# Layer 1's first nine hidden slices with their clip split between ScalarE and GpSimd, and a third score slot kept for one unit more

## The chip, the cores and the metric

The kernel runs on one core of a Trainium2 chip. The metric is device microseconds of one execution. The kernel before was timed three times: 1115.95 us is the median, 1115.87 and 1116.27 are the ends.

## The reference, cut to what matters

```python
# attention, 4 batches x 8 heads, 576 positions, head size 64
scores = scale * q @ k.T
scores = where(scores >= rowmax - tau, scores, -1e9)
attn   = softmax(scores)                  # then attn @ v, heads side by side: x is 2304 x 512
# layer 1, 512 -> 2048 -> 512
h = x @ w_in
g = where(h >= 1, h, where(h <= -1, 0, (h + 1) ** 2 / 4))
x = g @ w_out
# layer 2, 512 -> 2048 -> 512
r = maximum(x @ w_in2, 0);  g = s * r * r + b;  out = g @ w_out2
```

All is float32. Large matrix products are made of three passes over a high and a low part of each operand.

## The kernel before, in words

**Attention** is walked in 32 units: a unit is one half of the query rows of one pair of heads in one batch, so a batch has eight units, the four of the first half and then the four of the second. A unit of the first half has four score tiles (128 queries x 576 keys), one of the second half has five, so a batch has 36 tiles. For each tile TensorE makes the scores (line 515 in batches 0 and 1, where four matmuls run on quarters or halves of the array at once, called tiled below; line 524 in batches 2 and 3). VectorE takes the row minimum of the negated scores (570), ScalarE the exponential (573), VectorE masks and sums (578). The row sums go through some short instructions (591 to 597, on GpSimd or VectorE), one of GpSimd, VectorE and ScalarE normalises the tile (608, 613), TensorE transposes it (634, 650), ScalarE or VectorE copies it out (626, 627), and at the end of a row block the values are multiplied in (672, 673).

**Layer 1 beside attention.** The weights of ten of layer 1's sixteen slices of 128 hidden rows are brought in and split during the first 200 us: a chunk takes an Abs on ScalarE (816), a clamp on GpSimd (819), three bit operations on VectorE (822, 824, 826), a cast on ScalarE (828) and a subtraction on GpSimd (493). As soon as a group of 256 or 320 tokens has its attention output, some of its slices are computed between the score tiles: 3 for the first group, 7 for the second, then 10 for each of four more. A slice is twelve matmuls into a PSUM bank (898), the activation, a cast to the high part (918, ScalarE) and the low part (919, GpSimd); four output sums (941) use the slices of a group. The activation of a slice h is `c = clip(h, -1, 1)` on VectorE (906), `c = ((c + 1) / 2) ** 2` on ScalarE (908), `hs = max(c, h)` on VectorE (910).

**PSUM.** There are eight banks. Score tiles take two, as (0,1), (2,3) and, for the units below `ALONE`, (6,7) as well; these last two are `ps3_117` in the lists. Transposes and values use 4 and 5. From unit `ALONE` on, 6 and 7 are two banks of their own (`ps4_0`, `ps4_1`) for values, hidden slices and output sums. The first group's slices use them before that.

**Order.** Every operation is a task with a priority. A list scheduler in the kernel walks the tasks with its own costs and hop times, picks the engine where a task has alternatives, and writes the five engines' programs out in that order; on the chip each engine works through its list and waits where it has to. `OFF` shifts the priorities of the steps, `BURST` lets TensorE take several tasks of one kind in a row from the planned time `BURST_FROM` on. While TensorE has nothing to do in the plan, before 200 us, and one of the banks 4 to 7 is free, the scheduler puts in a fill: a matmul of the identity with itself (1092), whose result nobody reads.

**Afterwards** all that is left of layer 1 and then layer 2 runs with TensorE as the busy engine (898, 984, 1018).

Of the kernel before, what the change touches and what calls it, by code (L numbers as in the profile page):

```python
# [10 lines left out]
AF = mybir.ActivationFunctionType  # L11
ALU = mybir.AluOpType
# [17 lines left out]

WT0, WT = 0.0, 310.0

OFF = {"load": 0.0, "prep": 0, "qk": -8, "min": -3.0, "exp": -3, "mask": 0, "norm": 0, "trans": 3.58, "hi": 6, "av": 3, "xo": 0, "second": -12}
NSX, NSL, NV = 4, 5, 2

AHEAD = 1
# [12 lines left out]
QKW = 640 + S  # L49
NRH, NHH = 4, 3  # L50

ALONE = 6

BURST, BURST_FROM, BURSTS = 2, 200000.0, ("t", "r")
DMA_ISSUE, DMA_RATE, DMA_LAG = 475, 350.0, 2500.0

DMA_ALONE = 6000.0
# [41 lines left out]
class Sched:  # L99
# [14 lines left out]
    def add(self, alts, prio, r=(), w=(), group=None, lag=0, after=0.0):  # L114

        alts = [a + (True,) if a[0] == "pool" else a for a in alts]
        t = Task()
        t.alts, t.prio, t.idx, t.group, t.lag, t.after = alts, prio, len(self.tasks), group, lag, after
        t.succ, t.npred, t.ready, t.start, t.fn, t.preds = [], 0, 0.0, None, None, []
        preds = {}  # L120
        for k in r:
            p = self.lastw.get(k)
            if p is not None:
                preds[p.idx] = p
        for k in w:
            p = self.lastw.get(k)
            if p is not None:
                preds[p.idx] = p
            for p in self.readers.get(k, ()):
                preds[p.idx] = p  # L130
        for k in r:
            self.readers.setdefault(k, []).append(t)
        for k in w:
            self.lastw[k] = t
            self.readers[k] = []
        for p in preds.values():
            p.succ.append(t)
            t.npred += 1
        if group is not None:
            group.left += 1  # L140
        self.tasks.append(t)
        return t
# [154 lines left out]
def act_ns(n, bias=False):  # L297
    return 93 + n / 1.2 + (94 if bias else 0)
# [7 lines left out]
def dve_ns(n):  # L306
    return 68 + 1.0417 * n


def fast_ns(n):  # L310
    return 68 + 0.521 * n
# [6 lines left out]
def pfast_ns(n):  # L318
    return 60 + 1.07 * n
# [20 lines left out]
def attention_then_ffn(tc, qk, v, tau, w1, w2, s2, b2, out):  # L340
    nc = tc.nc
    sch = Sched()
    add = sch.add
# [538 lines left out]
    def hidden(f, T, xs, layer, cands, gs):  # L882
        pr = prio_f()
        g = Group(cands)
        kg = ("bank", g)
        i = tctr[0]
        tctr[0] += 1
        hs, c = hs_t[i % NH][:, 0:T], c_t[i % NH][:, 0:T]
        khs, kc = ("hs", i % NH), ("c", i % NH)

        def mm():
            o = bank[g.banks[0]][:, 0:T]
            n = 0
            for k in range(4):
                wh, wl = WH[f][:, k * 128:(k + 1) * 128], WL[f][:, k * 128:(k + 1) * 128]
                x_h, x_l = XH[xs][:, k * T:(k + 1) * T], XL[xs][:, k * T:(k + 1) * T]
                for a, x in ((wh, x_h), (wh, x_l), (wl, x_h)):
                    nc.tensor.matmul(o, a, x, start=(n == 0), stop=(n == 11))  # L898
                    n += 1

        add([("pe", 12 * mm_ns(T), mm, "r")], pr, r=["two"] + wkeys(f, 0) + [(t, xs, j) for t in ("XH", "XL") for j in range(4)], w=[kg, "hidden order"] + gs[0] + gs[1], group=g)
        fp = (-1,) + pr
        kgh, kgl, gh, gl = gs
        if layer == 1:

            add([("dve", dve_ns(T), lambda: nc.vector.tensor_scalar(  # L906
                out=c, in0=bank[g.banks[0]][:, 0:T], scalar1=1.0, scalar2=-1.0, op0=ALU.min, op1=ALU.max))], fp, r=[kg], w=[kc], group=g)
            add([("act", act_ns(T, True), lambda: nc.scalar.activation(out=c, in_=c, func=AF.Square, bias=half, scale=0.5))],  # L908
                fp, r=[], w=[kc])
            add([("dve", dve_ns(T), lambda: nc.vector.tensor_tensor(out=hs, in0=c, in1=bank[g.banks[0]][:, 0:T], op=ALU.max))],  # L910
                fp, r=[kc, kg], w=[khs], group=g)
        else:
            add([("act", actp_ns(T), lambda: nc.scalar.activation(out=hs, in_=bank[g.banks[0]][:, 0:T], func=AF.Relu))],  # L913
                fp, r=[kg], w=[khs], group=g)
            add([("act", act_ns(T), lambda: nc.scalar.activation(out=c, in_=hs, func=AF.Square))], fp, r=[khs], w=[kc])  # L915
            add([("dve", fast_ns(T) + 122, lambda: nc.vector.tensor_scalar(out=hs, in0=c, scalar1=s_c, scalar2=b_c, op0=ALU.mult, op1=ALU.add))],  # L916
                fp, r=[kc, "sb"], w=[khs])
        add([("act", act_ns(T), lambda: nc.scalar.copy(out=gh, in_=hs))], fp, r=[khs], w=kgh)  # L918
        add([("pool", pool_ns(T), lambda: nc.gpsimd.tensor_tensor(out=gl, in0=hs, in1=gh.bitcast(F32), op=ALU.subtract)),  # L919
             ("dve", dve_ns(T), lambda: nc.vector.tensor_tensor(out=gl, in0=hs, in1=gh.bitcast(F32), op=ALU.subtract), True)],  # L920
            fp, r=[khs] + kgh, w=kgl)
# [243 lines left out]
```

## Time and profile before

| | |
|---|---|
| median of three runs | 1115.95 us |
| the profiled execution's own time | 1116.18 us |
| its span, first to last instruction | 1114.3 us |
| around the span | 1.9 us |
| busy: PE, PEld, DVE, ACT, POOL | 1099.0, 978.0, 621.0, 723.8, 603.7 us |
| chain that ended last | PE 87%, ACT 5%, DVE 5% |
| granted TensorE clock | 1.00 in all 40 slices |

PE is TensorE's matmuls, PEld its weight loads, DVE is VectorE, ACT is ScalarE, POOL is GpSimd. A row of the trace has a start and a length; an engine can start an instruction a little before the one ahead of it has ended, so on ScalarE and TensorE the distance between two starts, not the length, is what an instruction costs. A float32 matmul that is not split into parts stands as two records, so each fill of the program is two rows of the trace.

### The profile page before, as it was taken

To read this page: it belongs to the slowest core of one execution; us is meant where nothing else is said; L and a number is where in the kernel's file an instruction comes from. 1 tells how busy PE (TensorE), PEld (TensorE's weight loads), DVE (VectorE), ACT (ScalarE), POOL (GpSimd) and SP (SyncE) were. 2 spreads that over 40 slices of the span, in tenths; PEclk is the share of its full clock that TensorE was granted. 3 is DMA by queue.
4 is the path that set the end of the run, shared out by engine and by line. 5 is a ranking of instruction groups with operands and counts; after the bars stand their busy time and mean duration, and the time that the engine had idled before them with its cause. 6 is when DMAs were issued, how large, how long until landed. Compare 5 with 4: busy or idle time off the path is not lost.

```text
span 1114.3 us, 21581 instructions
## 1 busy us (share of the span) xinstructions
PE 1099.0 (99%) x7686; PEld 978.0 (88%) x7686; DVE 621.0 (56%) x1512; ACT 723.8 (65%) x1648; POOL 603.7 (54%) x954
## 2 busy tenths in 40 slices
PE   9899999999999999999999999999999999999998
PEld 6567777889888899899999999999999999999997
DVE  6998998778777665367888786761111111111111
ACT  6999898879877786456666655664544544445443
POOL 4666666778767473166777766772323323323222
PEclk9999999999999999999999999999999999999999
DMA  5645553354334321264456674410101101000000
GB/s 173 184 157 157 161 171 113 110 140 125 112 115 124 101 73 62 76 191 143 148 161 217 199 223 141 140 48 19 39 2 38 34 5 38 2 19 20 1 19 19
DMA packets 75850, 112.01 MB, mean 101 GB/s; under 512 B 7392, under 2 KB 44768, under 8 KB 75744
## 3 DMA queue, kind: packets, MB, share of 16 engines
q1 hardware_dynamic: 75744, 110.65, 32.2%
q8 instruction: 60, 0.98, 0.4%
q14 instruction: 46, 0.38, 0.1%
HBM read 87.03 MB, written 23.59 MB: 99 GB/s over the span
## 4 chain that ended last, share of the span: by engine, by line
PE 87%; ACT 5%; DVE 5%; issue 1%; POOL 1%; DMA 0%; ACTq 0%; POOLq 0%; DVEq 0%
PE ps L898 34%; PE ps L1018 18%; PE ps L984 11%; PE ps L941 7%; PE ps L672 5%; PE ps L634 4%; PE ps L524 3%; PE ps L515 2%; ACT p L613 2%; DVE p L578 1%; PE ps L673 1%; ACT e L573 1%; PE ps L1092 1%; ACT pt L626 1%; DVE stt L570 1%
## 5 line engine op out<-in xcount | busy, mean ns | idle before, releaser
L919 POOL TENSOR_TENSOR g<-hs,g 128x256 fp32r<-128x256 f32 (+1 forms) x272 | 214.1, 787 | 307.7 <-ACT g L918 285.4
L898 PE MATMUL ps<-xh,wh 128*128 128x256 f32 (+1 forms) x1088 | 316.4, 291 | 0.8 <-DVE hs L910 0.4
L898 PE MATMUL ps<-xl,wh 128*128 128x256 f32 (+1 forms) x1088 | 313.7, 288 | 0.0
L898 PE MATMUL ps<-xh,wl 128*128 128x256 f32 (+1 forms) x1088 | 313.7, 288 | 0.0
L916 DVE TENSOR_SCALAR hs<-c,cst 128x256 f32<-128x256 f32 x144 | 65.0, 451 | 313.5 <-ACT c L915 313.5
L898 PEld LDWEIGHTS ps<-xh,wh 128*128 128x128 f32 x1088 | 206.2, 189 | 9.3 <-DVE hs L910 1.6
L898 PEld LDWEIGHTS ps<-xl,wh 128*128 128x128 f32 x1088 | 206.1, 189 | 5.8
L898 PEld LDWEIGHTS ps<-xh,wl 128*128 128x128 f32 x1088 | 206.0, 189 | 0.0
L1018 PE MATMUL ps<-wh,g 128*128 128x512 f32 x576 | 202.9, 393 | 0.0
L918 ACT CAST g<-hs 128x256 fp32r<-128x256 f32 (+1 forms) x272 | 113.7, 418 | 92.1 <-DVE hs L916 62.1
L913 ACT ACTIVATE hs<-ps 128x256 f32<-128x256 f32 x144 | 55.4, 384 | 133.1 <-PE ps L898 131.8
L578 DVE SCALAR_TENSOR_TENSOR p<-ps,stt,e 128x576 f32<-128x576 f32 x144 | 116.0, 813 | 34.3 <-ACT e L573 18.1
L984 PE MATMUL ps<-g,wh 128*128 128x256 f32 (+1 forms) x624 | 127.4, 297 | 0.4 <-DVE ye L994 0.3
L1018 PEld LDWEIGHTS ps<-wh,g 128*128 128x128 f32 x576 | 108.6, 189 | 19.5
L493 POOL TENSOR_TENSOR wl<-wt,wh 128x256 fp32r<-128x256 f32 x128 | 101.2, 795 | 40.0 <-ACT wh L828 39.3
L570 DVE TENSOR_REDUCE stt<-ps 128x1 f32<-128x576 f32 x144 | 105.4, 749 | 22.3 <-PE ps L524 11.4
L1018 PE MATMUL ps<-wl,g 128*128 128x512 f32 x288 | 113.8, 395 | 0.0
L573 ACT ACTIVATE e<-ps,stt 128x576 f32<-128x576 f32 x144 | 105.4, 747 | 9.7 <-DVE stt L570 8.2
L613 ACT ACTIVATE p<-p,stt 128x576 f32<-128x576 f32 (+3 forms) x113 | 92.4, 822 | 22.2 <-DVE stt L597 20.4
L984 PEld LDWEIGHTS ps<-g,wh 128*128 128x128 f32 x624 | 100.0, 189 | 1.7 <-DVE ye L994 1.1
L908 ACT ACTIVATE c<-c,cst 128x320 f32<-128x320 f32 (+1 forms) x128 | 68.6, 537 | 50.4 <-DVE c L906 49.3
L984 PE MATMUL ps<-g,wl 128*128 128x256 f32 (+1 forms) x312 | 92.0, 295 | 0.0
(71 smaller groups left out, 1962.3 us busy)
## 6 DMA issues: line engine op xcount, KB each, us to landing
st<-in_w_dram SPq DMA_DIRECT2D x128, 256.0 KB, 3.7
vr<-in_v_dram SPq DMA_DIRECT2D x32, 320.0 KB, 3.2
r<-in_qk_dram SPq DMA_DIRECT2D x32, 288.0 KB, 2.9
xr<-xT SPq DMA_DIRECT2D x8, 640.0 KB, 6.0
r<-in_qk_dram SPq DMA_DIRECT2D x16, 304.0 KB, 3.9
xr<-y1T SPq DMA_DIRECT2D x9, 512.0 KB, 3.8
out_dram<-yo SPq DMA_DIRECT2D x18, 256.0 KB, 2.0
r<-in_qk_dram SPq DMA_DIRECT2D x16, 272.0 KB, 3.2
```

The source lines that it names most:

```text
L493: return [("pool", pool_ns(n), lambda: nc.gpsimd.tensor_tensor(out=o(), in0=x(), in1=y(), op=op)), ("dve", dve_ns(n), lambda: nc.vector.te ...
L570: add([("dve", 665, lambda: nc.vector.tensor_reduce(out=nm[:, x:x + 1], in_=Sv(), axis=AX.XY, op=ALU.min))], at(pr, "min"), r=[kg], w=[ks[ ...
L573: add([("act", 624, lambda: nc.scalar.activation(out=ev, in_=Sv(), func=AF.Exp, bias=nm[:, x:x + 1], scale=-1.0))], at(pr, "exp"), r=[kg, ...
L578: nc.vector.scalar_tensor_tensor(out=p[:, x * S:x * S + S].rearrange("p (a c) -> p a c", a=2), in0=Sv(), scalar=nthr[:, x:x + 1], in1=ev, ...
L613: nc.scalar.activation(out=p[i:j, o:o + w], in_=p[i:j, a:a + w], func=AF.Identity, scale=rc[i:j, x:x + 1], bias=un[i:j, x:x + 1])
L898: nc.tensor.matmul(o, a, x, start=(n == 0), stop=(n == 11))
L908: add([("act", act_ns(T, True), lambda: nc.scalar.activation(out=c, in_=c, func=AF.Square, bias=half, scale=0.5))], fp, r=[], w=[kc])
L918: add([("act", act_ns(T), lambda: nc.scalar.copy(out=gh, in_=hs))], fp, r=[khs], w=kgh)
L919: add([("pool", pool_ns(T), lambda: nc.gpsimd.tensor_tensor(out=gl, in0=hs, in1=gh.bitcast(F32), op=ALU.subtract)), ("dve", dve_ns(T), lam ...
L941: nc.tensor.matmul(o, a[:, c], x, start=(f == 0 and n == 0), stop=(f == nf - 1 and n == 2))
L984: nc.tensor.matmul(o, a[:, c], x, start=(f == f0 and n == 0), stop=(f == f1 - 1 and n == 2))
L1018: nc.tensor.matmul(o, x[:, c], a[:, 512:1024], start=(f == 0 and n == 0), stop=(f == NF - 1 and n == 2))
```

## The change

Four things change. In the first nine hidden slices (three of the first token group, six of the seven of the second) the activation becomes `c = relu(h / 2 + 1 / 2)` on ScalarE straight from PSUM, `c = min(c, 1)` on GpSimd (or VectorE, which the scheduler takes for none of the nine), `c = c ** 2` on ScalarE, and the same maximum as before on VectorE. `ALONE` goes from 6 to 7, so unit 6 also has the third score slot. The values' priority is shifted by 5.75 places in place of 3. Bursts of the kind "r" (hidden slices, output sums, scores of batches 2 and 3) begin at 100 us of the plan in place of 200.

```diff
-OFF = {..., "trans": 3.58, "hi": 6, "av": 3, "xo": 0, "second": -12}
+OFF = {..., "trans": 3.58, "hi": 6, "av": 5.75, "xo": 0, "second": -12}
-ALONE = 6
+ALONE = 7
+LIGHT = 9
-BURST, BURST_FROM, BURSTS = 2, 200000.0, ("t", "r")
+BURST, BURST_FROM, BURSTS = 2, 100000.0, ("t","r")
...
-            add([("dve", dve_ns(T), lambda: nc.vector.tensor_scalar(
-                out=c, in0=bank[g.banks[0]][:, 0:T], scalar1=1.0, scalar2=-1.0, op0=ALU.min, op1=ALU.max))], fp, r=[kg], w=[kc], group=g)
-            add([("act", act_ns(T, True), lambda: nc.scalar.activation(out=c, in_=c, func=AF.Square, bias=half, scale=0.5))],
-                fp, r=[], w=[kc])
+            if tctr[0] <= LIGHT:
+                add([("act", act_ns(T, True), lambda: nc.scalar.activation(
+                    out=c, in_=bank[g.banks[0]][:, 0:T], func=AF.Relu, bias=half, scale=0.5))], fp, r=[kg], w=[kc], group=g)
+                add([("pool", pfast_ns(T), lambda: nc.gpsimd.tensor_scalar(out=c, in0=c, scalar1=1.0, scalar2=1.0, op0=ALU.min, op1=ALU.mult)),
+                     ("dve", fast_ns(T), lambda: nc.vector.tensor_scalar(out=c, in0=c, scalar1=1.0, scalar2=None, op0=ALU.min), True)],
+                    fp, r=[], w=[kc])
+                add([("act", act_ns(T), lambda: nc.scalar.activation(out=c, in_=c, func=AF.Square))], fp, r=[], w=[kc])
+            else:
+                ...  # the two lines removed above
             add([("dve", dve_ns(T), lambda: nc.vector.tensor_tensor(out=hs, in0=c, in1=bank[g.banks[0]][:, 0:T], op=ALU.max))],
                 fp, r=[kc, kg], w=[khs], group=g)
```

The four together let the scheduler write another order from the fifth unit on. Three places show it. In the lists of the changed kernel line numbers are 2 higher than before up to the activation (517 for 515, 636 for 634) and 11 higher behind it (952 for 941, 1103 for 1092).

TensorE in units 5 and 6 of batch 0, before: `ps_117` (banks 6 and 7) goes from the scores to the first hidden slice, between the scores of unit 5 and those of unit 6.

```order
L650 MATMUL ps_1_113<-ident,p_121 128x128
L1092 MATMUL ps_0_112<-ident 128x128 x2
L898 MATMUL ps_117<-xh_89,wh_69 128x256
...
L672 MATMUL ps_0_112<-pt,vr_135 64x320 x8
L673 MATMUL ps_0_112<-pl,vr_135 128x320
L634 MATMUL ps_1_113<-ident,p_122 128x128 x4
L515 MATMUL ps_0_110<-r_131 128x288 x2
L515 MATMUL ps_1_111<-r_132 128x288 x2
L898 MATMUL ps_117<-xh_89,wh_70 128x256
```

The same place in the changed kernel:

```order
L652 MATMUL ps_1_113<-ident,p_121 128x128
L1103 MATMUL ps_0_112<-ident 128x128 x2
L517 MATMUL ps_117<-r_131 128x288 x2
L674 MATMUL ps_0_112<-pt,vr_135 64x320 x8
L675 MATMUL ps_0_112<-pl,vr_135 128x320
L636 MATMUL ps_1_113<-ident,p_122 128x128 x4
L517 MATMUL ps_0_110<-r_132 128x288 x2
L517 MATMUL ps_1_111<-r_131 128x288 x2
L636 MATMUL ps_0_112<-ident,p_122 128x128 x4
```

The third slot takes a score tile of unit 6, and the three slices of the first token group (36 matmuls of line 898) stand some twenty rows later, among the scores of units 6 and 7; the sums that use them move with them.

TensorE at the first scores of batch 1 (unit 8), before: fills stand between transposes and scores.

```order
L634 MATMUL ps_1_113<-ident,p_122 128x128 x4
L1092 MATMUL ps_1_1056<-ident 128x128 x5
L650 MATMUL ps_0_112<-ident,p_122 128x128
L1092 MATMUL ps_1_1056<-ident 128x128
L634 MATMUL ps_1_113<-ident,p_120 128x128 x4
L1092 MATMUL ps_1_1056<-ident 128x128 x2
L634 MATMUL ps_0_112<-ident,p_120 128x128 x4
L1092 MATMUL ps_1_1056<-ident 128x128 x2
L515 MATMUL ps_0_110<-r_132 128x288 x2
L515 MATMUL ps_1_111<-r_131 128x288 x2
L650 MATMUL ps_0_112<-ident,p_120 128x128
L1092 MATMUL ps_1_1056<-ident 128x128 x9
```

The same place in the changed kernel:

```order
L952 MATMUL ps_117<-g_93,wl_79 128x256
L517 MATMUL ps_1_111<-r_131 128x288 x2
L952 MATMUL ps_117<-g_94,wh_70 128x256 x2
L952 MATMUL ps_117<-g_94,wl_80 128x256
L952 MATMUL ps_117<-g_95,wh_71 128x256 x2
L952 MATMUL ps_117<-g_95,wl_81 128x256
L1103 MATMUL ps_1_113<-ident 128x128
L1103 MATMUL ps_117<-ident 128x128 x2
L636 MATMUL ps_0_112<-ident,p_121 128x128 x4
L652 MATMUL ps_1_113<-ident,p_121 128x128
L1103 MATMUL ps_1_1156<-ident 128x128 x6
L517 MATMUL ps_0_110<-r_132 128x288 x2
```

The output sums of the first group stand where fills stood. Over the whole list of TensorE the fills go from 66 to 43 and no other kind of matmul changes its number.

ScalarE at the first slices, before (`c0_102` to `c2_104` are the slices' buffers):

```order
L828 CAST wh1_70<-wt0_146 128x256
L908 ACTIVATE c0_102<-c0_102,cst_68 128x256
L828 CAST wh1_70<-wt1_147 128x256
L918 CAST g0_93<-hs0_99 128x256
L453 ACTIVATE r2_133<-r2_133 128x320
```

In the changed kernel:

```order
L910 ACTIVATE c0_102<-ps3_117,cst_68 128x256
L628 COPY pt_137<-ps1_0_112 128x4x128
L628 COPY pl_138<-ps1_1_113 128x128
L575 ACTIVATE e0_118<-ps2_0_110,stt1_124 128x576
L915 ACTIVATE c0_102<-c0_102 128x256
L910 ACTIVATE c1_103<-ps3_117,cst_68 128x256
L830 CAST wh3_72<-wt0_146 128x256
L830 CAST wh3_72<-wt1_147 128x256
L915 ACTIVATE c1_103<-c1_103 128x256
```

Where one ScalarE instruction of a slice stood ahead of its cast there are now two, with GpSimd's minimum between them.

## Rows read from the trace of the kernel before

**Rows 1.** Windows: us, then busy PE, PEld, DVE, ACT, POOL, clock, DMA.
```profile
20.50:41.00 20.50, 18.36 (x129) 11.63 (x130) 19.58 (x50) 19.86 (x43) 12.87 (x27) 1.00 0.55 175
41.00:66.30 25.30, 23.38 (x164) 14.13 (x161) 24.17 (x66) 23.90 (x52) 17.27 (x36) 1.00 0.58 168
66.30:95.60 29.30, 28.21 (x204) 19.41 (x202) 26.84 (x71) 25.67 (x59) 18.14 (x35) 1.00 0.44 136
95.60:176.60 81.00, 80.89 (x584) 61.91 (x580) 73.31 (x199) 74.70 (x158) 50.80 (x99) 1.00 0.55 166
176.60:204.70 28.10, 28.01 (x220) 21.89 (x218) 25.43 (x66) 23.46 (x54) 17.92 (x33) 1.00 0.24 69
204.70:475.00 270.30, 266.85 (x2005) 240.15 (x2002) 178.83 (x459) 207.30 (x410) 170.29 (x255) 1.00 0.37 108
475.00:1114.30 639.30, 634.61 (x4295) 594.83 (x4293) 261.29 (x580) 337.27 (x855) 307.52 (x445) 1.00 0.25 81
```

**Rows 2.** Row minima: count, ns min/median/max, first and last start, three windows from 0.
```profile
L570 DVE TENSOR_REDUCE stt<-ps x18: 729/752/759, 8.4 to 41.0; 128x1 f32<-128x576 f32 x18
...
L570 DVE TENSOR_REDUCE stt<-ps x36: 729/748/759, 8.4 to 95.6; 128x1 f32<-128x576 f32 x36
...
L570 DVE TENSOR_REDUCE stt<-ps x72: 729/748/759, 8.4 to 204.7; 128x1 f32<-128x576 f32 x72
```

**Rows 3.** The fills' line: count, ns min/median/max, first and last start.
```profile
L1092 PE MATMUL ps<-ident x132: 270/275/579, 1.3 to 198.7; 128*128 128x128 f32 x132
```

**Rows 4.** Timeline of TensorE: start, us, line, operation, count.
```profile
64.55 1.24 PE L515 MATMUL ps<-r 64*128 64x288 f32 x8
65.72 0.39 PE L898 MATMUL ps<-xh,wh 128*128 128x256 f32 x1
...
69.85 0.76 PE L515 MATMUL ps<-r 64*128 64x288 f32 x4
70.54 1.09 PE L634 MATMUL ps<-ident,p 128*128 128x128 f32 x8
71.57 0.76 PE L515 MATMUL ps<-r 64*128 64x288 f32 x4
...
82.76 0.40 PE L941 MATMUL ps<-g,wh 128*128 128x256 f32 x2
83.00 0.28 PE L941 MATMUL ps<-g,wl 128*128 128x256 f32 x1
...
101.42 2.17 PE L1092 MATMUL ps<-ident 128*128 128x128 f32 x18
103.43 0.60 PE L634 MATMUL ps<-ident,p 128*128 128x128 f32 x4
```

**Rows 5.** Groups by line, 41:204.7: count, busy us, mean ns, idle before.
```profile
L613 ACT ACTIVATE p<-p,stt 128x576 f32<-128x576 f32 (+3 forms) x43 | 34.8, 811 | 3.6 <-DVE stt L597 3.2
L626 ACT COPY pt<-ps 128x512 f32<-128x512 f32 x51 | 28.6, 589 | 2.6 <-PE ps L634 2.5
L828 ACT CAST wh<-wt 128x256 fp32r<-128x256 f32 x35 | 13.8, 417 | 0.6 <-DVE wt L826 0.5
L908 ACT ACTIVATE c<-c,cst 128x256 f32<-128x256 f32 (+1 forms) x20 | 10.5, 529 | 0.0
...
L824 DVE SCALAR_TENSOR_TENSOR wt<-st,wt 128x256 uint32<-128x256 uint32 x34 | 17.1, 508 | 0.0
L906 DVE TENSOR_SCALAR c<-ps 128x256 f32<-128x256 f32 (+1 forms) x20 | 8.8, 441 | 2.6 <-PE ps L898 2.5
...
L819 POOL TENSOR_SCALAR wt<-wt 128x256 f32<-128x256 f32 x34 | 14.1, 425 | 6.0 <-ACT wt L816 4.6
```

**Rows 6.** Timeline of ScalarE: two instructions, one behind the other.
```profile
91.27 0.40 ACT L828 CAST wh<-wt 128x256 fp32r<-128x256 f32 x1
91.58 0.45 ACT L816 ACTIVATE wt<-st 128x256 f32<-128x256 f32 x1
```

**Rows 7.** Line 822 on VectorE, 20:205: count, ns min/median/max, first and last start.
```profile
L822 DVE TENSOR_SCALAR wt<-wt x39: 270/285/843, 23.0 to 197.2; 128x256 uint32<-128x256 uint32 x39
```

More of the change, by code (lines that the diff above doesn't have):

```diff
@@ L31 @@
 WT0, WT = 0.0, 310.0
-OFF = {"load": 0.0, "prep": 0, "qk": -8, "min": -3.0, "exp": -3, "mask": 0, "norm": 0, "trans": 3.58, "hi": 6, "av": 3, "xo": 0, "second": -12}
+OFF = {"load": 0.0, "prep": 0, "qk": -8, "min": -3.0, "exp": -3, "mask": 0, "norm": 0, "trans": 3.58, "hi": 6, "av": 5.75, "xo": 0, "second": -12}
 NSX, NSL, NV = 4, 5, 2
@@ L904, in hidden @@
         if layer == 1:
-            add([("dve", dve_ns(T), lambda: nc.vector.tensor_scalar(
-                out=c, in0=bank[g.banks[0]][:, 0:T], scalar1=1.0, scalar2=-1.0, op0=ALU.min, op1=ALU.max))], fp, r=[kg], w=[kc], group=g)
-            add([("act", act_ns(T, True), lambda: nc.scalar.activation(out=c, in_=c, func=AF.Square, bias=half, scale=0.5))],
-                fp, r=[], w=[kc])
+            if tctr[0] <= LIGHT:
[6 more added lines that the diff above has]
+            else:
+                add([("dve", dve_ns(T), lambda: nc.vector.tensor_scalar(
+                    out=c, in0=bank[g.banks[0]][:, 0:T], scalar1=1.0, scalar2=-1.0, op0=ALU.min, op1=ALU.max))], fp, r=[kg], w=[kc], group=g)
+                add([("act", act_ns(T, True), lambda: nc.scalar.activation(out=c, in_=c, func=AF.Square, bias=half, scale=0.5))],
+                    fp, r=[], w=[kc])
             add([("dve", dve_ns(T), lambda: nc.vector.tensor_tensor(out=hs, in0=c, in1=bank[g.banks[0]][:, 0:T], op=ALU.max))],
```

## The prediction

> **What bounds the kernel now.** I read windows cut where attention's work can be counted first, then TensorE's and ScalarE's timelines, then groups by line. The windows show two regimes [rows 1]. From 204.7 us to 475 us TensorE is idle for 3.5 us, from there to the end for 4.7 us, and VectorE (66%, then 41%) and ScalarE (77%, then 53%) have room. Before 204.7 us VectorE and ScalarE are at 84% to 97% while TensorE looks busy too: between 95.6 and 204.7 us it is idle for 0.2 us. That last number deceives. Part of the work is fills: 132 records, all begun by 198.7 us [rows 3], which are 66 matmuls. Eighteen records run from 101.42 to 103.43 us [rows 4], so a fill matmul costs 0.223 us, and all fills 14.7 us. What a change before 204.7 us can win is therefore fills and idle TensorE time; all other matmuls must be done anyway, and what is late at 204.7 us is late at the end.
>
> The cuts are the 18th, 36th and 72nd row minimum, at 41.0, 95.6 and 204.7 us [rows 2]: the middle and the end of batch 0 and the end of batch 1. Against them I count what each engine's list holds before and after.
>
> **TensorE's sum.** 23 fills fewer: 23 x 0.223 = -5.1 us. The lists also differ in how often TensorE goes over to the tiled scores of batches 0 and 1: 50 visits become 53. A visit with eight records takes 1.17 us to the next start (64.55 to 65.72), one with four 0.69 (69.85 to 70.54), so four records are 0.48 and 0.21 us go with leaving; the eight transposes behind take 1.03 us, where eight records at a fill's spacing of 0.112 would take 0.90 [rows 4]. A visit costs 0.34 us, three of them +1.0. TensorE's list is 4.1 us shorter. This becomes time only where TensorE is not made to wait instead.
>
> By the last score of batch 0 the lists differ by -4.9 us (eight fills fewer ahead of it, -1.8; 33 matmuls of the output sums, at the 0.12 us between 82.76 and 83.00 for two of them [rows 4], move behind it, -3.9; four transposes come ahead, +0.9), by the last of batch 1 by -4.1: no hidden slice or sum stands on another side of that cut. So batch 1 has 0.8 us more on TensorE than before, batch 0 has 4.9 less.
>
> **The activation itself.** Nine clips leave VectorE: 9 x 0.44 = -4.0 us [rows 5]. ScalarE's first instruction now reads PSUM with the scale and bias that its square had, so I price it like that square (0.53 us long); the plain square is new and is priced like a cast of the same tile (0.42). On ScalarE neighbours overlap by 0.09 us (91.27 + 0.40 against 91.58) [rows 6], which makes the new one 0.33 us of its time: 9 x 0.33 = +3.0. GpSimd gets nine minima, priced like the clamp of the weights, 0.43 us: +3.8. No row shows this Relu or this minimum; the bounds are 0.29 to 0.72 us a piece (a cast's spacing less its overlap, and a normalisation's), which is +2.6 to +6.5 for nine and no gain. GpSimd is busy 62% to 68% of these windows [rows 1], so its part hides; what it costs where it does not is a rival below. The chain of a slice has one hop more, and the output sums wait for it; they stand some twenty rows later than the slice in TensorE's list, and I cost the hop at nothing.
>
> **What attention allows.** From the 18th to the 27th minimum (41.0 to 66.3 us) no slice of layer 1 is left in the changed lists. ScalarE's loses two normalisations, two Abs of weights, a square and a cast: 2 x 0.72 + 4 x about 0.36 (between the cast's 0.33 and the square's 0.44) = -2.9; VectorE's loses six instructions of 0.44 to 0.51: -2.7 [rows 5]. That leaves 21.0 and 21.5 us. The window ahead of it, also without slices, shows the share that they reach then: 19.86 of 20.50, 97% [rows 1]. 21.5 / 0.97 = 22.2 where 25.3 were: -3.1 us. From the 27th to the 36th ScalarE gets 2.9 us more (three normalisations, two more of the activation's instructions than before plus three squares, a copy out, less three casts and three copies of sums): 28.6, at 97% 29.5 us where 29.3 were, +0.2. VectorE has less than before. So the 36th minimum can come 2.9 us earlier, not 4.9: TensorE gets 2.0 us of waits that no fill shows, because in this stretch the scores hold banks 6 and 7. If ScalarE stays at its shares of before (94% and 88%), the 36th comes 0.2 later and the waits are 5.1.
>
> **The sum.** -4.1 + 2.0 = -2.1 us, nothing behind 204.7 us, where TensorE's list is the same in work and the others have room. On the profiled 1116.18 us that gives 1114.1; the median of the runs stands 0.2 lower, so 1113.9 us. The other edits (values later by 2.75 places, bursts from 100 us) are in the lists already and cost nothing beyond them.
>
> **Rivals.**
>
> *TensorE's sum alone.* The fills sat in stalls which the new order closes, and the waits in batch 0 do not come or the 3.0 us of idle time between 41.0 and 95.6 us shrink along. For it: with ScalarE at 97% and VectorE at 96% at once the window to 41.0 us shows that the engines can run so tight. Against it: TensorE had little to do there. It gives -4.1 us, 1111.9, and with the idle time gone as well -6, 1110.
>
> *Attention keeps its pace in batch 0.* The shares stay at 94% and 88%; the fills that vanish are replaced by waits. -4.1 + 5.1 = +1.0, 1117.0 us. The Trainium skill (Perfetto Trace Analysis, Identifying the Most-Contended Engine) says that matmul busy time is a bad measure and weight-load time the better one. By it, with PEld at 56% to 76% in the windows up to 176.6 us, TensorE would not be the limit there, its shorter list would be worth nothing, and time would be this rival's. The trace agrees for the fills and not for the rest: the starts in [rows 4] follow at a matmul's own pace.
>
> *ScalarE becomes the bound in batch 1* (the slower side). Between the 36th and the 72nd minimum ScalarE's list grows: six squares, five normalisations from GpSimd, five copies out from VectorE, four other instructions net. 6 x 0.33 + 5 x 0.72 + 5 x up to 0.50 + 4 x 0.33 = 8 to 9 us, on 98.2 of 109.1 us [rows 1, 5]. To be done in the same time it would have to be busy 98%; with the 2.9 us won ahead the point from which the kernel loses is about 95.5%. At 97%, 110.6 us, the gain falls to 1.4; at 94.5%, the share of the window to 66.3 us, 113.4 us stand for 109.1, the sum is +1.4; at the 92% of the window to 176.6 us +4.5, 1120.4. Centre +3, 1118.9. Against it: some of these instructions only stand ahead of the 72nd exponential in place of behind it, and there ScalarE had 17% to spare.
>
> *GpSimd's minima block VectorE.* An in-place VectorE instruction on SBUF of 0.285 us median took up to 0.843 [rows 7]: something holds it for up to 0.56 us, about as long as a GpSimd instruction. Nine minima of 0.43 us could hold VectorE for 3.9 us, all of the clips' saving; where that falls on the path the sum is -2.1 + 3.9 = +1.8, and 1118 with five short instructions more that VectorE takes over in batch 1. The Trainium skill (SBUF — State Buffer, SBUF: two separate sides) says that GpSimd and VectorE in its two-port forms share a port pair which one of them holds for a whole instruction. By it each minimum is such a lock, and the clip from PSUM that it replaces was none, so the change would lose on VectorE what it saves. The trace shows such a length, and not what held them.
>
> **How the numbers follow.** Less than 0.2%, about 2.2 us, can't be told from no change. The sum above 0.40, its own range -1.0 to -3.3; it lies at the edge, so 0.18 of it is faster and 0.22 within. TensorE's sum alone 0.25, faster. Attention at its pace 0.14, within. ScalarE bound in batch 1 0.16 and GpSimd's block 0.05, slower. Faster 0.43, same 0.36, slower 0.21. The range leaves out the best part of the first rival and the worst of ScalarE's: 1110.9 to 1118.8 us.
>
> **What would show it.** 86 records of fills, and the 36th minimum near 92.7 us with more TensorE idle time between 50 and 75 us, for the step on batch 0. ScalarE at 95% or more between the 36th and the 72nd minimum and the 72nd at 202 to 203 us for batch 1. Relu near 0.53 us, the minimum near 0.43 for the prices. The sum is wrong if TensorE idles beyond 95.6 us, if the 36th minimum stays at 95 us, or if the stretch behind the 72nd changes by more than a microsecond.

## The result and the profile after

The changed kernel took 1125.32 us (median of four runs, 1123.16 to 1126.84), the kernel before 1115.91 (four runs, 1114.80 to 1116.27). The ratio is 1.0086, 95% interval 1.0074 to 1.0099: slower by 0.86%, outside the range of 1110.9 to 1118.8. The profiled execution took 1126.5 us with a span of 1124.5.

The windows of the changed kernel at the cuts of [rows 1]; columns: us, then busy PE, PEld, DVE, ACT, POOL, clock, DMA.

```profile
41.00:66.30 25.30, 22.69 (x155) 12.99 (x152) 24.82 (x67) 23.41 (x50) 17.80 (x37) 1.00 0.59 176
66.30:95.60 29.30, 24.65 (x151) 15.42 (x149) 20.58 (x59) 24.34 (x54) 17.27 (x30) 0.88 0.29 90
95.60:176.60 81.00, 75.92 (x529) 57.76 (x530) 67.39 (x179) 69.44 (x150) 54.80 (x93) 1.00 0.54 164
176.60:204.70 28.10, 27.28 (x210) 20.56 (x209) 24.88 (x66) 26.54 (x59) 17.91 (x33) 1.00 0.27 86
204.70:475.00 270.30, 266.67 (x1997) 237.60 (x1997) 185.28 (x475) 214.36 (x431) 171.97 (x253) 1.00 0.35 103
```

TensorE was idle for 1.1 us between 66.3 and 95.6 us and for 0.1 us between 95.6 and 176.6; it is idle for 4.7 and 5.1 now. VectorE and ScalarE lose busy time in the same two windows, 12.2 and 6.6 us together. So no engine became the bound: all of them wait. And the granted clock of the first one is 0.88, where it was 1.00.

The fills and the row minima, against [rows 2, 3]; columns: count, ns min/median/max, first and last start.

```profile
L1103 PE MATMUL ps<-ident x86: 270/275/582, 1.3 to 152.3; 128*128 128x128 f32 x86
...
L572 DVE TENSOR_REDUCE stt<-ps x18: 732/752/758, 8.0 to 40.6; 128x1 f32<-128x576 f32 x18
L572 DVE TENSOR_REDUCE stt<-ps x27: 732/748/758, 8.0 to 62.2; 128x1 f32<-128x576 f32 x27
L572 DVE TENSOR_REDUCE stt<-ps x36: 731/747/758, 8.0 to 97.2; 128x1 f32<-128x576 f32 x36
L572 DVE TENSOR_REDUCE stt<-ps x72: 728/748/758, 8.0 to 219.9; 128x1 f32<-128x576 f32 x72
```

There are 86 fill records where there were 132, as counted. The 27th minimum starts at 62.2 us, 4.1 us earlier than before: that part came. Then nine minima take 35.0 us where they took 29.3, and the 72nd is 15.2 us late. Of these, 5.0 come back: 39 matmuls that stood behind it (15 of the output sums, 10 of the values, 8 transposes and others) have run by then, and the rest takes 904.6 us for 909.6. 10.2 us of span remain.

What the three new instructions took, and the waits between 66 and 150 us (columns: what waits, for what, us in total, times, longest).

```profile
L910 ACT ACTIVATE c<-ps,cst x9: 452/511/545, 80.2 to 136.8; 128x320 f32<-128x320 f32 x6, 128x256 f32<-128x256 f32 x3
L912 POOL TENSOR_SCALAR c<-c x9: 1067/1297/1358, 80.8 to 138.0; 128x320 f32<-128x320 f32 x6, 128x256 f32<-128x256 f32 x3
L915 ACT ACTIVATE c<-c x9: 416/470/473, 81.9 to 139.3; 128x320 f32<-128x320 f32 x6, 128x256 f32<-128x256 f32 x3
```

```profile
ACT c L915 <- POOL c L912: 4.2, 7, 1.1
...
DVE p L580 <- ACT e L575: 7.1, 9, 1.8
DVE hs L921 <- ACT c L915: 4.0, 4, 1.6
...
PE ps L517 <- DVE p L580: 2.5, 4, 1.0
PE ps L636 <- ACT pt L628: 2.1, 5, 1.0
PE ps L1103 <- DVE hs L921: 1.3, 1, 1.3
PE ps L952 <- ACT c L910: 1.2, 1, 1.2
```

ScalarE's Relu and square cost what was assumed (0.51 and 0.47 us). GpSimd's minimum takes 1.07 to 1.36 us, three times the 0.43 it was priced at. One reading is that its lateness goes round: the square waits for it (4.2 us), the exponentials queue behind the square, VectorE waits for the exponentials (7.1 us, 2.4 in the kernel before), TensorE for VectorE's bank. Of these links only the first is shown to hang on the minimum's length: with a short pair of operations (the first experiment) the square waits 0.3 us, and VectorE still waits 7.5 us for the exponentials.

The place of the first two slices, in timelines of ScalarE, GpSimd and TensorE; columns: start, length, line, operation, count, and in brackets the idle time ahead and what ended it.

```profile
76.81 2.16 ACT L615 ACTIVATE p<-p,stt 64x64 f32<-64x64 f32 x3
80.20 0.47 ACT L910 ACTIVATE c<-ps,cst 128x256 f32<-128x256 f32 x1 [1.23 <-PE ps L900]
80.57 0.58 ACT L628 COPY pt<-ps 128x512 f32<-128x512 f32 x1
...
82.21 0.46 ACT L910 ACTIVATE c<-ps,cst 128x256 f32<-128x256 f32 x1
...
83.88 0.42 ACT L915 ACTIVATE c<-c 128x256 f32<-128x256 f32 x1 [0.61 <-POOL c L912]
```

```profile
80.76 1.10 POOL L912 TENSOR_SCALAR c<-c 128x256 f32<-128x256 f32 x1 [2.07 <-ACT c L910]
82.75 1.09 POOL L912 TENSOR_SCALAR c<-c 128x256 f32<-128x256 f32 x1 [0.90 <-ACT c L910]
```

```profile
77.90 0.29 PE L900 MATMUL ps<-xh,wl 128*128 128x256 f32 x1
...
79.88 0.28 PE L900 MATMUL ps<-xh,wl 128*128 128x256 f32 x1
81.20 1.09 PE L636 MATMUL ps<-ident,p 128*128 128x128 f32 x8 [1.04 <-ACT pt L628]
...
87.48 0.51 PE L952 MATMUL ps<-g,wh 128*128 128x256 f32 x2 [1.22 <-ACT c L910]
...
87.95 0.27 PE L652 MATMUL ps<-ident,p 128*128 128x128 f32 x1
89.54 0.80 PE L1103 MATMUL ps<-ident 128*128 128x128 f32 x2 [1.32 <-DVE hs L921]
90.13 1.06 PE L636 MATMUL ps<-ident,p 128*128 128x128 f32 x4
91.12 4.47 PE L674 MATMUL ps<-pt,vr 128*64 128x320 f32 x16
```

The first slice's last matmul ends at 78.19 us, and ScalarE is free from 78.97. Its Relu starts at 80.20, 0.04 us after the end of the *second* slice's last matmul (79.88 + 0.28). Meanwhile GpSimd has nothing to do, because its list stands at the minimum (2.07 us), and the copy behind the Relu on ScalarE makes TensorE wait 1.04 us. At 87.48 an output sum waits for the third slice's Relu, though the sum writes bank 7 and the Relu reads bank 6, and at 89.54 a fill, whose result nobody reads, holds TensorE for 1.32 us until the third slice's maximum has read its bank. The granted clock falls at 88.6 us, within the last of these idle stretches (88.22 to 89.54).

Two windows of the kernel before, of the changed one, of the one without the nine activations and of the one with the first three alone (both below), in this order; columns as above.

```profile
74.00:88.60 14.60, 14.13 (x102) 9.74 (x101) 13.70 (x35) 12.33 (x28) 8.56 (x17) 1.00 0.55 175
88.60:95.40 6.80, 6.45 (x45) 3.65 (x47) 5.76 (x17) 6.24 (x16) 3.94 (x7) 1.00 0.45 118
```

```profile
74.00:88.60 14.60, 11.80 (x82) 8.66 (x78) 10.02 (x29) 12.10 (x26) 10.67 (x17) 1.00 0.31 90
88.60:95.40 6.80, 5.86 (x22) 2.97 (x22) 3.44 (x10) 4.59 (x12) 3.83 (x7) 0.50 0.09 33
```

```profile
74.00:88.60 14.60, 13.58 (x101) 9.56 (x99) 12.64 (x34) 14.01 (x31) 9.33 (x17) 1.00 0.34 109
88.60:95.40 6.80, 6.77 (x50) 5.33 (x51) 5.57 (x17) 6.31 (x14) 5.98 (x13) 1.00 0.69 219
```

```profile
74.00:88.60 14.60, 10.85 (x77) 8.30 (x75) 9.39 (x25) 12.07 (x28) 9.74 (x15) 1.00 0.32 98
88.60:95.40 6.80, 6.80 (x50) 4.10 (x50) 5.29 (x14) 5.85 (x13) 4.35 (x9) 1.00 0.27 81
```

For 6.8 us TensorE has 1.2 GHz (0.50) in place of 2.4 and does 22 matmuls where it did 45; before that it was idle for 2.8 of 14.6 us, against 0.5 in the kernel before. The amount of idle time does not decide by itself: in the last two rows TensorE was idle for 3.75 of the 14.6 us and the clock stayed at 1.00, while four other runs of that kernel have a mean clock of 0.997. So that the idle stretches brought the clock down is likely, but not shown. The sixteen value matmuls at 91.12 take 4.47 us; before, such a group took 2.38. The two runs of the changed kernel whose mean clock was 0.996 took 1126.5 and 1126.8 us, the one at 1.000 took 1123.2, and 1124.1 at 0.998 lies between: the lower clock is about 3.5 us of the loss, in the runs that have it.

### The profile page after: what moved, and what is told of

The parts are those of the page before. It is cut to its first block, busy times and chain, and to the rows that moved or that the text cites. A ratio compares the mean times of both kernels' runs of the same rounds, so it can differ in the third digit from the quotient of the medians.

```text
span 1124.5 us, 21525 instructions
## 1 busy us (share of the span) xinstructions
PE 1099.0 (98%) x7640; PEld 974.1 (87%) x7640; DVE 619.1 (55%) x1508; ACT 729.8 (65%) x1667; POOL 612.7 (54%) x948
## 4 chain that ended last, share of the span: by engine, by line
PE 81%; ACT 8%; DVE 6%; POOL 2%; issue 2%; ACTq 0%; DVEq 0%; POOLq 0%
PE ps L900 32%; PE ps L1029 18%; PE ps L995 11%; PE ps L952 6%; PE ps L674 4%; PE ps L636 3%; ACT p L615 2%; PE ps L517 2%; DVE p L580 2%; PE ps L526 2%; ACT e L575 2%; ACT pt L628 2%; DVE stt L572 1%; PE ps L675 1%; PE ps L1103 1%
## 5 line engine op out<-in xcount | busy, mean ns | idle before, releaser
L580 DVE SCALAR_TENSOR_TENSOR p<-ps,stt,e 128x576 f32<-128x576 f32 x144 | 116.1, 813 | 34.6 <-ACT e L575 22.2
L575 ACT ACTIVATE e<-ps,stt 128x576 f32<-128x576 f32 x144 | 105.3, 749 | 11.7 <-DVE stt L572 10.5
L615 ACT ACTIVATE p<-p,stt 128x576 f32<-128x576 f32 (+3 forms) x110 | 89.8, 820 | 18.9 <-DVE stt L599 17.8
L919 ACT ACTIVATE c<-c,cst 128x320 f32<-128x320 f32 (+1 forms) x119 | 63.9, 537 | 54.1 <-DVE c L917 53.2
```

Of the source, the lines that this page charges most:

```text
L575: add([("act", 624, lambda: nc.scalar.activation(out=ev, in_=Sv(), func=AF.Exp, bias=nm[:, x:x + 1], scale=-1.0))], at(pr, "exp"), r=[kg, ...
L580: nc.vector.scalar_tensor_tensor(out=p[:, x * S:x * S + S].rearrange("p (a c) -> p a c", a=2), in0=Sv(), scalar=nthr[:, x:x + 1], in1=ev, ...
L615: nc.scalar.activation(out=p[i:j, o:o + w], in_=p[i:j, a:a + w], func=AF.Identity, scale=rc[i:j, x:x + 1], bias=un[i:j, x:x + 1])
```

## The experiments

The theory formed from these rows: the nine activations lose the time and the other edits do not; of the loss one part is the minimum's length, another the new place of the chain on ScalarE and GpSimd. Rivals: the new order alone; ScalarE's added work; GpSimd as such. A caution for all of them: each kernel with another table or price is planned anew as a whole. The four lists here that have none of the new activations and the third slot for six or seven units run at 1113.7, 1115.0, 1115.9 and 1117.1 us, so between such kernels a difference under some 3 us decides nothing. The kernel before, run beside each experiment, had medians of 1114.9 to 1116.0 us, so two experiments' medians can differ by 1 us from that alone; their ratios to the kernel before are free of it.

**The minimum's second operation.** The changed kernel with (minimum, maximum with 0) on GpSimd, which computes the same; no other instruction, place or planned cost differs.

```diff
-  scalar1=1.0, scalar2=1.0, op0=ALU.min, op1=ALU.mult
+  scalar1=1.0, scalar2=0.0, op0=ALU.min, op1=ALU.max
```

> The changed kernel with GpSimd's instruction as min(c, 1) then max(., 0), in place of min(c, 1) then times 1: the same result and the same order of every engine, only another pair of operations. Theory 1 (the pair min-then-times is slow on GpSimd, 1.07 to 1.36 us where 0.43 was priced, and ScalarE's square, VectorE's maximum and what is queued behind them wait for it): the instruction falls to 0.40 us at 256 columns and 0.49 at 320, the clock stays at full speed, and the time is 1112 to 1116 us. Theory 2 (the hop through ScalarE and GpSimd costs the time whatever the instruction's length): 1119 to 1123 us, with the instruction short. Theory 3 (the new order of the other three edits costs it): 1119 to 1124 us.

1120.22 us (1118.10 to 1122.39), ratio 1.0045 [1.0028, 1.0062]. The instruction now takes 0.399 to 0.510 us. So 5 of the 9.4 us hang on the length of nine instructions on an engine that is busy 54% of the time. The time lies above the first theory's 1112 to 1116: the rest has another cause. Part of the 5 can be the clock, since this trace has 3.4 us at 1.2 GHz where the changed kernel's has 6.8; the fastest runs of the two, both at a clock of 1.000, took 1118.1 and 1123.2 us.

To see whether it is the second operation or the multiply, one kernel gave each of the nine another pair; the eighth (multiply, multiply) leaves the clip at 1 out.

```diff
+PAIRS = [min*mult, min*max, max*min, mult*min, min*add, add*min, min*min, mult*mult, min*max]
-  op0=ALU.min, op1=ALU.mult
+  op0=oa, op1=ob      # pair number tctr[0] - 1
```

> The changed kernel with another pair of operations in GpSimd's instruction for each of the nine slices, in this order: min-mult, min-max, max-min, mult-min, min-add, add-min, min-min, mult-mult, min-max. The eighth leaves the clip at 1 out. One look, for the price of each. If the pair as such decides (theory 1), min-mult takes 1.07 us at 256 columns and min-max 0.40, and the rest fall to one or the other group; a pair that is slow at 320 columns takes 1.30 to 1.36. If the place in the program decides (what VectorE does beside it), the pairs do not matter and all nine lie near 1.1 and 1.3 us. Time 1114 to 1124 us.

One run, 1125.55 us. The nine rows on GpSimd, in the order of the list of pairs (L917 is the minimum's line there).

```profile
80.98 1.10 POOL L917 TENSOR_SCALAR c<-c 128x256 f32<-128x256 f32 x1 [2.10 <-ACT c L915]
82.98 0.40 POOL L917 TENSOR_SCALAR c<-c 128x256 f32<-128x256 f32 x1 [0.89 <-ACT c L915]
87.72 1.08 POOL L917 TENSOR_SCALAR c<-c 128x256 f32<-128x256 f32 x1 [0.41 <-ACT c L915]
118.04 1.31 POOL L917 TENSOR_SCALAR c<-c 128x320 f32<-128x320 f32 x1 [0.48 <-ACT c L915]
120.36 1.31 POOL L917 TENSOR_SCALAR c<-c 128x320 f32<-128x320 f32 x1 [0.31 <-ACT c L915]
126.03 1.34 POOL L917 TENSOR_SCALAR c<-c 128x320 f32<-128x320 f32 x1 [0.97 <-PE ps L520]
128.37 1.29 POOL L917 TENSOR_SCALAR c<-c 128x320 f32<-128x320 f32 x1 [0.25 <-ACT c L915]
137.00 0.52 POOL L917 TENSOR_SCALAR c<-c 128x320 f32<-128x320 f32 x1
137.74 0.45 POOL L917 TENSOR_SCALAR c<-c 128x320 f32<-128x320 f32 x1 [0.22 <-ACT c L915]
```

(Minimum, maximum) and (multiply, multiply) are short, 0.40 us on 128 x 256 and 0.45 to 0.52 on 128 x 320. (Maximum, minimum), with the same two operations in the other order, takes 1.08 us on 128 x 256, and the other pairs take 1.29 to 1.34 on 128 x 320. The price goes by the pair, and neither by the multiply nor by the tile. For (maximum, minimum) the constants 1 and 0 change places with the operations, so that the order of the operations alone does it is not shown.

**The order edits without the activations.**

```diff
-LIGHT = 9
+LIGHT = 0
```

> The changed kernel with LIGHT at 0: the nine slices have VectorE's clip again; third slot for unit 6, values' priority and bursts stay as changed. Theories 1 and 2 (the nine activations cost the time): 1113 to 1117 us. Theory 3 (the order of the other edits costs it): 1121 to 1125 us.

1113.65 us (1112.81 to 1115.25, ten runs), ratio 0.9990 [0.9980, 0.9999]: the lowest median of this study, 1.3 us under the 1114.93 of the kernel before beside it. The interval ends just under 1, and by the caution above this is no sure gain. So the order edits are not the loss. The fills fall from 18.1 to 11.5 us, summed from the start of each to the next start on TensorE.

```profile
66.30:95.60 29.30, 27.49 (x197) 18.88 (x196) 25.55 (x71) 28.18 (x62) 19.05 (x37) 1.00 0.45 142
95.60:176.60 81.00, 79.60 (x568) 61.40 (x567) 75.39 (x196) 71.42 (x157) 51.75 (x97) 1.00 0.53 165
```

TensorE's idle time in these two windows is 1.2 us in the kernel before, 3.2 here and 9.7 in the changed kernel: a part of what the fills give back is waited for.

The parts of it alone: the third slot for unit 6, and the values' shift with the bursts.

```diff
-ALONE = 6
+ALONE = 7
```

> The kernel before with ALONE at 7 alone: the third score slot for one unit more. The three edits together, without the nine activations, gave 1113.65 us, 1.3 under the kernel before on the same chip. If the third slot is what gains: 1112 to 1114 us. If it is the values' priority or the bursts: 1114.5 to 1117 us.

1115.03 us, 0.9995 [0.9985, 1.0004]: no difference.

```diff
-"av": 3  ...  BURST_FROM = 200000.0
+"av": 5.75  ...  BURST_FROM = 100000.0
```

> The kernel before with the values' shift 5.75 and the bursts from 100 us alone: the third score slot as before (6), no new activation. The slot alone moved the time by -0.05%, the three order edits together by -0.1%. If the gain of the three is the values' shift and the bursts, this one comes to 1113 to 1115; if it needs the third slot with them, it stays at 1115 to 1117.

1117.09 us, 1.0010 [1.0002, 1.0019]. No part gains alone, and what the three gain together is too little to be told from the scatter between lists.

**The activations without the order edits**, with the long and with the short minimum.

```diff
 # the kernel before, and only
+LIGHT = 9
```

> The kernel before with the nine activations of the changed kernel alone: ALONE 6, values' shift 3, bursts from 200 us of the plan. Theories 1 and 2: 1121 to 1126 us, with GpSimd's minimum at 1.07 us or more and idle time on ScalarE in front of the squares. Theory 3: 1115 to 1118 us.

1125.74 us, 1.0094 [1.0077, 1.0111], granted clock 1.00: the whole loss, in another order and with no drop of the clock. In this order the 36th minimum starts at 95.6 us, as in the kernel before, and the matmul records ahead of it are the same but for 16 fills and two scores fewer, some 2 us. The first three slices are among them, so here no more than those 2 us are lost up to that point.

> The kernel before with the nine activations alone, GpSimd's instruction as min then max: the same order as the run with the nine activations alone and the slow pair (1125.7 us). If the slow pair costs about the same in this order as in the changed one (5.1 us): 1119 to 1122 us. If the loss there, most of which shows between 230 and 290 us, hangs on the order and not on the instruction: 1123 to 1126 us.

1120.96 us, 1.0051 [1.0034, 1.0067]. The short pair takes 4.8 us off here and 5.1 there, so in two lists that were both planned for a short minimum the long one costs about the same.

**Two other chains of the same length.** A hop is the step from one engine to the next. The activation before has two, the changed one three, and both of these have three as well. First the minimum on VectorE, behind ScalarE's Relu; then VectorE starts the chain (h/2 + 1/2 from PSUM), GpSimd clips with the short pair, ScalarE squares. The two cuts below give the instructions in short.

```diff
-  ("pool", ..., gpsimd min, mult) or ("dve", ..., min)
+  ("dve", ..., min)
```

> The changed kernel with the minimum on VectorE alone: Relu on ScalarE from PSUM, min(c, 1) on VectorE, square on ScalarE, maximum on VectorE; the scheduler knows, so the order is another one. What is left of the loss once GpSimd's instruction is short (5 us of it went with the short pair) is 6.6 us against the version without the nine activations. Theory A (the Relu stands in ScalarE's queue behind instructions of 0.6 to 0.9 us, starts 0.5 to 2 us after its slice, and holds the PSUM bank and VectorE's maximum for that long): 1117 to 1121 us. Theory B (any further hop in the chain costs it, wherever): 1117 to 1121 us too. Theory C (GpSimd's part, short or not): 1113 to 1116 us.

1116.70 us, 1.0013 [1.0004, 1.0023].

```diff
-  act: Relu(h / 2 + 1 / 2);  pool: min, mult
+  dve: h * 0.5 + 0.5;        pool: min, max
```

> The changed kernel with VectorE in front again and GpSimd kept: c = h / 2 + 1 / 2 on VectorE from PSUM, clip to 0 and 1 on GpSimd (min then max), square on ScalarE, maximum on VectorE. The chain has as many hops as the changed kernel's, ScalarE has one instruction of a slice as before. Theory A (ScalarE's queue in front of the Relu): 1113 to 1116 us, with the first instruction within 0.5 us of its slice's end. Theories B and C (the hop, or GpSimd): 1117 to 1121 us.

1116.63 us, 1.0009 [1.0000, 1.0018]. Both times lie between the ranges that the theories had set. Over the kernel without the activations the two cost 3.0 us each by the medians, 2.6 and 2.1 by the ratios, which is at the edge of what can be told; the changed chain with the short pair costs 6.6, or 6.1 by the ratios. So neither ScalarE's added work (the first has all of it), nor GpSimd as such (the second has it), nor the number of hops (three in all of them) is the loss by itself. That it adds up along the chain is not shown.

**The length, or a list written for another length.** The planner priced the minimum at 60 + 1.07 ns a column, 0.33 us. Here it plans 4.1 ns a column; the chip's instruction stays as long as it was.

```diff
-  add([("pool", pfast_ns(T), ... gpsimd min, mult), ("dve", ...)], ...)
+  add([("pool", 4.1 * T, ... gpsimd min, mult)], ...)
```

> The changed kernel with one number and one alternative different: the nine minima stay on GpSimd with minimum and multiply, but the scheduler plans 4.1 ns a column for them (1.05 and 1.31 us, what the trace of the changed kernel shows) where it planned 60 + 1.07 a column (0.33 and 0.40 us), and has no VectorE alternative. The chip's instruction is as long as before; only the lists differ. Theory lists (the loss is an order written for a minimum of a third of its length: ScalarE's square stands at the head of its list, waits up to 1.1 us for GpSimd, and the exponentials queue behind it): with the square placed later the time falls to that of the short pair, 1120 us or less, 1118 if the order also takes the waits of ScalarE for GpSimd (4.2 us between 66 and 150 us) away whole. Theory length (the chain slice, Relu, minimum, square, maximum, sums is itself too long, wherever its parts stand): within 1.5 us of the changed kernel, 1124 to 1127.

1120.43 us, 1.0047 [1.0035, 1.0059], 0.4 over the range of the theory of the lists and 3.6 under that of the length. The same long minimum, and the time of the short one; the wait of ScalarE's square for GpSimd is no longer among ScalarE's waits, which were led by its 4.2 us. The same length costs 5 us less in a list that knows of it. So what costs is not the 0.7 to 0.9 us by which each minimum is longer, but a list that was planned without them. Which of the waits in that list carries the loss is not shown: the square's own wait does not measure it, since the kernel with the last six activations (below) has 3.3 us of that wait between 66 and 150 us and loses little, and the one with the first three has 0.9 and loses most.

**Which slices.** The new activation for the first three alone, and for the last six alone.

```diff
-LIGHT = 9
+LIGHT = 3
```

> The changed kernel with the new activation for the first three slices alone (the first token group, computed in batch 0), planned anew; the six of the second group keep VectorE's clip and the scaled square. With nine the time is 1125.3, with none 1113.7. Theory by number (each activation costs alike, 11.7 / 9 = 1.3 us): 1117.6. Theory batch 0 (the three stand where the slices share banks 6 and 7 with the scores, and TensorE's waits between 75 and 100 us grew by 7 to 8 us, against 4.7 between 125 and 150 us): 1120 to 1122. Theory batch 1 (the six carry it, since ScalarE has least room there): under 1116.

1125.45 us, 1.0080 [1.0065, 1.0094]: all of the loss with a third of the activations, and above every range that was set. Two runs at a granted clock of 0.999 or more took 1121.8 and 1122.1, four at 0.997 took 1125.4 to 1125.9.

```diff
-  if tctr[0] <= LIGHT:
+  if 3 < tctr[0] <= LIGHT:
```

> The mirror of the kernel with three: the first three slices keep VectorE's clip and the scaled square, the six of the second group have the new activation with its long minimum, planned anew. Theory first three (the cost arises where the first group's slices share banks 6 and 7 with the score tiles, in batch 0): 1113.5 to 1116.5 us, TensorE's granted clock 1.00 throughout, its waits between 75 and 100 us back at about 2.5 us. Theory by number (each new activation costs alike): 6 x 1.3 on 1113.7 = 1121.5. If the first three cost 8 to 12 and the six still cost 4 or more when they stand alone, the two costs overlap and neither place is the cause by itself.

1116.87 us, 1.0012 [1.0003, 1.0021], 0.4 over the first theory's range and 4.6 under the other's. The three of batch 0 cost 11.8 us over the kernel with none (10.0 by the ratios), about 3.5 of them by the clock; the six of batch 1 cost 3.2 alone (2.5). Their sum exceeds the loss of the nine by 2 to 3 us, too little to say whether the costs overlap. And this place belongs to the changed order: with the activations alone in the order before, no more than 2 us were lost by the end of batch 0.

**Why the first three.** Their slices and sums use banks 6 and 7 while these are one tile, `ps3_117`; the six have `ps4_0` and `ps4_1`. In ScalarE's list the second Relu has no wait for TensorE of its own, though nothing between the two waits for TensorE:

```
140 L910 ACTIVATE c0_102<-ps3_117,cst_68 128x256 [waits PE_49]
141 L628 COPY pt_137<-ps1_0_112 128x4x128 [waits DVE_49]
...
144 L915 ACTIVATE c0_102<-c0_102 128x256 [waits Pool_49]
145 L910 ACTIVATE c1_103<-ps3_117,cst_68 128x256
```

So the first one's wait covers the second slice. This delays the first Relu; that the delay makes the loss does not follow. The kernel with the minimum on VectorE has it too, with the same wait of TensorE behind the copy, and costs only the 2.1 to 3.0 us found above:

```profile
79.96 0.47 ACT L910 ACTIVATE c<-ps,cst 128x256 f32<-128x256 f32 x1 [1.24 <-PE ps L900]
...
80.96 1.09 PE L636 MATMUL ps<-ident,p 128*128 128x128 f32 x8 [1.04 <-ACT pt L628]
```

The kernel with `ALONE = 3` gives the first three slices two tiles; read as a pair, with and without the activations.

```diff
-ALONE = 7
+ALONE = 3        # and, in the second kernel of the pair, LIGHT = 0
```

> The changed kernel with ALONE = 3 in place of 7: the third score slot ends before the first hidden slice, so banks 6 and 7 are two tiles of their own (ps4_0, ps4_1) when the first group's three slices and their sums use them; all nine new activations stay, with the long minimum. It is read against the next kernel, which has the same slot without the new activations; the slot's loss for units 3 to 6 moves both. Theory shared tile (the first three slices cost 8 us because banks 6 and 7 are one tile to the program's waits: the first Relu waits for the second slice's last matmul, a sum and a fill wait for the third slice's readers, and ScalarE's copies stand behind): each Relu now waits for its own slice, the three gaps of 1.6 to 2.1 us ahead of it fall under 1 us where ScalarE is free, and the pair's difference is at most 6 us. Theory place (it is the place in batch 0 and the length of the chain, whatever the tile): the difference stays at 9 to 13 us, as 1125.3 against 1113.7 with ALONE = 7.

> The same with none of the new activations (LIGHT = 0): the base of the pair. With the third slot for fewer units attention starts slower: 1114 to 1122 us.

1122.90 us, 1.0074 [1.0061, 1.0086], and 1117.24, 1.0022 [1.0013, 1.0031]. The difference is 5.7 us where it was 11.7 (10.7 by the ratios). The first three Relus now:

```profile
53.99 0.47 ACT L910 ACTIVATE c<-ps,cst 128x256 f32<-128x256 f32 x1
...
58.29 0.47 ACT L910 ACTIVATE c<-ps,cst 128x256 f32<-128x256 f32 x1
...
60.26 0.49 ACT L910 ACTIVATE c<-ps,cst 128x256 f32<-128x256 f32 x1
```

Their slices end at 53.96, 57.21 and 59.53 us, so the gaps are 0.04, 1.08 and 0.73 us where they were 2.01, 2.05 and 1.64. The pair's difference came out as the shared tile had it, narrowly (5.7, under the 6 that was set), and one gap stays over the 1 us that was set. The tile's share of the 6 us is not isolated: the slot's end moves the first three slices some 25 us earlier and among other work. And the first kernel of the pair still has 6.8 us at the lower clock, from 63.4 and from 135.1 us on.

## Why the prediction was wrong, step by step

**The activation itself: the step that failed.** "GpSimd gets nine minima, priced like the clamp of the weights, 0.43 us", with bounds of 0.29 to 0.72, and "its part hides". It measured 1.07 to 1.36, and it did not hide. The clamp was the nearest row by engine and tile, but the changed kernel's minimum has another pair of operations, and the short pair shows that the clamp's price would have held for a clamp. The planner had the same kind of price, 0.33 us, and its lists were wrong with it. This is 5 of the 9.4 us.

"The chain of a slice has one hop more ... I cost the hop at nothing", since the sums stand some twenty rows later. One sum waited, 1.2 us, and not for its own slice's hop but for another slice's Relu on the shared tile; TensorE's other waits in the rows above were for other work on ScalarE and VectorE and, 1.3 us, for a maximum ahead of a fill. From the end of a slice's matmuls to the end of its maximum the mean of the nine went from 2.5 to 4.6 us. That mean is no measure of the loss: with the true price it is 4.5, at 1120.4 us. With the short pair 6 to 7 us are left over the kernel without the activations, two other chains with as many hops cost 2 to 3, and in the runs that have the lower clock about 3.5 us go with it; these parts overlap. What in the changed chain makes up this rest stays open: the shared tile delays the first Relu, and its share is not isolated. The prediction knew that the clip from PSUM went to ScalarE; it did not ask what ScalarE has in its list ahead of it and behind.

**ScalarE's own price was right.** Relu 0.51 for 0.53, square 0.47 for 0.42. The rival of ScalarE as the bound named the right side with the wrong mechanism: ScalarE is at 86% between 95.6 and 176.6 us (69.44 of 81.00), less than the 92% before, because it waits.

**TensorE's sum.** Fills 86 records, as counted. The condition that was put on it, "this becomes time only where TensorE is not made to wait instead", decided: between 66.3 and 176.6 us its idle time rises from 1.2 to 9.7 us. All three of the prediction's own signs of being wrong came: TensorE idles 5.1 us between 95.6 and 176.6 us, the 36th minimum starts at 97.2 us, later still than before, and the stretch behind the 72nd changed by 5.0 us. Without the activations the idle time there rises to 3.2 and the gain is 1.3 us, within the sum's range of -1.0 to -3.3. That sum was worked out on the lists with the activations, and 1.3 us can hardly be told from none, so the agreement is not more than luck. Two terms were also added up wrong, by far less than the miss: four transposes are 0.5 us by [rows 4] where 0.9 was taken, and -4.1 with 3.0 us of idle time gone is -7.1 where -6 was taken.

**What attention allows.** "21.5 / 0.97 = 22.2 where 25.3 were": from the 18th to the 27th minimum 21.6 us were needed. Right. From there to the 36th 29.5 were forecast; 35.0 were needed with the activations. The kernel without them has its 36th at 86.4 us.

**GpSimd's minima block VectorE.** The VectorE instructions that overlap the nine minima in time took 0.7 us more in all than the medians of their lines and shapes, nearly all of it in three of line 828 (0.61 to 0.67 us for 0.42). A loss of 3.9 us is not borne out, though the minima were three times as long as thought. The Trainium skill's port rule (SBUF — State Buffer, SBUF: two separate sides) would hold such an instruction for the whole of a minimum. The trace does not show that: the three are 0.2 us longer, and a fourth, inside a minimum at 118.49 us, took its usual 0.42. By the Trainium skill's weight-load rule (Perfetto Trace Analysis, Identifying the Most-Contended Engine) the prediction had a shorter list of TensorE worth nothing here. Without the activations it was worth 1.3 us at most, which agrees; the loss is not in that rule, since the time went into waits on all engines at once.

## What to carry to other kernels

Price an instruction of GpSimd by a row with the same pair of operations in the same order, not by the same engine and tile. Where no row has it, the longest row of that size is no bound: it was 1.03 us for GpSimd on 128 x 256 in the kernel before, and the minimum took 1.07 to 1.10. One kernel with a different pair in each place shows the prices of all. When a step moves to another in-order engine, list what stands behind it there: that work waits too, and a planner that is told a third of an instruction's length writes a list that loses time, here 5 us, which the same instruction did not lose in a list planned for its length. Two tenants of one tile can wait for each other even when they use different banks. And where every kernel is planned anew, a cause that was found in one order (here the first three slices) has to be looked for again in another.

## What the runs showed of the hardware that was not expected

GpSimd's two-operation instruction on a 128 x 256 float32 tile takes 0.40 us for (minimum, maximum) and 1.07 to 1.10 us for (maximum, minimum) and (minimum, multiply); on 128 x 320 it takes 0.45 to 0.52 against 1.29 to 1.36. And 2.8 us of idle TensorE in 14.6, in pieces of at most 1.3 us, were followed by 6.8 us at 1.2 GHz in the middle of a kernel that had kept 2.4 until then; the kernel without the activations, with 1.0 us idle there (13.58 of 14.60 busy), kept it. So did one execution with 3.75 us idle there, of the kernel with the first three activations, whose other runs have mean clocks down to 0.997: the same list can lose the clock in one run and keep it in the next.
